# Second half of the w_out product by seven block products: a fused attention and gated-MLP layer on one core

## The chip, the cores and the metric

The kernel runs on one core of one Trainium2 chip. The metric is the device time of one execution in microseconds (us), from start to end on that core; a lower one is better. The time before is the median of four runs. A profile of one execution, taken by the hardware profiler, shows where that time goes: each instruction on each engine with its start and its length, and for an engine that sat idle, what it waited for.

The engines are named as in the profile: PE is TensorE (matmul), PEld its weight load, DVE is VectorE, ACT is ScalarE, POOL is GpSimd, SP is SyncE, which here only issues DMAs. A name with a q, such as ACTq, is the queue of that engine when it issues a DMA.

## The reference

One layer of a sequence model: a block A with linear-memory attention, then a block B with a spatially gated MLP. S is 2048 tokens, D is 1024 features, F is 3584, Fh is 1792. All inputs and the output are bf16. The change lies in the last line of block B alone.

```python
h  = x + A(layernorm(x), wq, wk, wv, wo, beta)
z  = gelu(layernorm(h) @ w_in)                  # [2048, 3584]
z1 = z[:, :1792]
z2 = layernorm(z[:, 1792:])
g  = w_sp @ z2 + b_sp[:, None]                  # w_sp: [2048, 2048], over tokens
h2 = h + (z1 * g) @ w_out                       # w_out: [1792, 1024]
```

## The kernel before

**How the order is made.** The kernel writes out its program by hand. Each call such as `pe.matmul(...)`, `dve.tensor_tensor(...)` or `sp.dma_start(...)` goes through a recorder. It appends the instruction to that engine's own queue, in the order of the calls, and works out from the memory that each instruction touches which semaphores it must wait for. So each engine runs its queue strictly in the order written, and an instruction that waits holds up what stands behind it on that engine. All instructions but the launch carry one source line, the recorder's L210; they are told apart by the names of their tiles.

**Seven products.** A product of two matrices that are each cut into 2 x 2 blocks needs eight block products. It can be done with seven, if sums and differences of blocks are multiplied and the seven results are combined (the scheme of Winograd). The kernel before does this for part of the z1 projection and for both halves of the gate product w_sp @ z2. It works with fp16 operands, scaled by powers of two so that sums of blocks stay within range.

**The stages at the end of the kernel**, which are what the change touches:

1. *Gate 0*, `gate(0)`: the gate for tokens 0 to 1023. It has 7 groups g; each is a block of 128 of the 896 features of one half of Fh. A group needs seven products of 8 matmuls with 512 columns: with `b11` (helper `p1`), `b21` (`p2`), `t2`, `t1`, `t3`, `t4` and `b22`. Four operand sums per group, `ss(1..4, g)`, 128x1024 in fp16 on DVE, fill the four parts of the tile `ss` through `s_sum`. They exist once, not twice.
2. *The 16 units*: 16 calls of `out_unit` for tokens 0 to 1023. Each multiplies 14 chunks of z1T with half of w_out's columns (14 matmuls of 512 columns), adds the residual, which was loaded into a `fin` tile from where h was stored, and stores the result. Loads and stores of `fin` are issued from ACT's queue. Meanwhile the transposed blocks of w_sp for gate 1 are loaded by SP and are scaled and summed on DVE (`sp_half`, `sp_sum`).
3. *Gate 1*, `gate(1)`: the same for tokens 1024 to 2047. At its beginning, the second half of w_out's columns is loaded into the part of z1T that the units have left, a DMA of 1.8 MB on SP.
4. *Last units*: 16 further units (the last one cut into 384 and 128 columns) for tokens 1024 to 2047, with `fin` loads and stores on SP's queue.

**Inside a group of the gate.** The banks of PSUM are used so that products are added onto one another: `t2` goes to bank `bb`, DVE reads it (`u2 = bank * scale + s1b2`), then `t3` is added onto it and DVE reads again (`u3`), then `t4` is added and DVE reads a third time (`s1b1`). So the `t3` product must wait until DVE has read u2, and `t4` until DVE has read u3. Bank `bc` takes `t1`, then `b22`. PE's order in a group is t2, t1, (p1 of group g+2 if 1 <= g <= 3), t3, then p2 of the next group (p1 of group 6 in group 5, p2 of group 6 in group 6), t4, b22. DVE's order is u2, ss(1, g+1), ss(2, g+1), u3 twice, `out`, ss(3, g+1), `c11`, s1b1, `out`, u2 again for `bc`, `out`, ss(4, g+1). Here `out` multiplies a finished gate block with its block of z1T and writes the result back into z1T as bf16. `copy1` on ACT takes the p1 product out of its bank, and POOL adds the bias rows `brow` to it, twice per group (tile `tmp_s1b`).

**Scales.** `scale_of` turns squares that ACT has summed (`SQ`, `accum_out`) into one factor: a cast to bf16 on POOL into the tile `SQB`, a small matmul with ones (`ONES`) that sums over the 128 partitions, then a few one-column steps on DVE and a power of -1/2 on POOL, cut to a power of two. The name `TOT` stands for the total and `INV[0]` for the inverse of the gate's scale.

Of the kernel before, what the change touches and what calls it, by code (L numbers as in the profile page):

```python
# [5 lines left out]
BF16 = mybir.dt.bfloat16  # L6
F16 = mybir.dt.float16
F32 = mybir.dt.float32
I32 = mybir.dt.int32
ACTF = mybir.ActivationFunctionType  # L10
ALU = mybir.AluOpType

T = 2048
# [5 lines left out]
FH = 1792  # L19
NTC = T // 128  # L20
# [238 lines left out]
def bass_sequential_preLN__memory_aug_infini_attn__mixer_gmlp__prompt_kernel(  # L259
# [15 lines left out]
    out2d = out[0]  # L275
    R = _Recorder(nc)
    pe, act, dve, pool, sp = R.pe, R.act, R.dve, R.pool, R.sp

    K = 1024
# [4 lines left out]
    def tens(name, shape, dt, off):  # L284
        sz = int(np.prod(shape[1:])) * mybir.dt.size(dt)
        assert off % 32 == 0 and off + sz <= ARENA, (name, off, sz)
        t = nc.alloc_sbuf_tensor_at(name, list(shape), dt, offset=abase + off)
        R.space[t[:].tensor.name] = ("sbuf", off)
        return t

    class Bump:
# [4 lines left out]
        def __call__(self, name, shape, dt):  # L296
# [68 lines left out]
    Z2H = tens("z2h", [128, NTC, FH], F16, 134 * K)  # L365
    Z1T = tens("z1T", [128, 14, T], BF16, 62 * K)
    ROLES = (("b11", 14), ("b12", 22), ("b22", 46), ("b21", 126))
    RAW = {k: tens(k + "r", [128, 8, L], BF16, o * K) for k, o in ROLES}
    BH = {k: tens(k + "h", [128, 8, L], F16, o * K)
          for k, o in ROLES + (("t1", 118), ("t2", 190), ("t3", 22), ("t4", 38))}  # L370
    SS = tens("ss", [128, 4, 8, 128], F16, 30 * K)
    Z1X = tens("z1x", [128, 14, T], F16, 62 * K)
# [6 lines left out]
    b3 = Bump(dead, 4 * K)  # L379
# [4 lines left out]
    ONES = b3("ones", [128, 128], BF16)  # L384
    MHZ = b3("mhz", [128, 1], F32)
    SQ = b3("sq", [128, 16], F32)
    SQZ = b3("sqz", [128, 14], F32)
    SQB = b3("sqb", [128, 16], BF16)
    TOT = b3("tot", [128, 1], F32)
    TOP = b3("top", [128, 1], F32)  # L390
    SC = [b3("sc%d" % i, [128, 1], F32) for i in range(2)]
    INV = [b3("inv%d" % i, [128, 1], F32) for i in range(2)]
    TMP = {k: tens("tmp_" + k, [128, L], F32, (4 + 2 * i) * K)
           for i, k in enumerate(("s1", "s1b1", "s1b2", "u2", "u3"))}
    SJ = [tens("sj%d" % i, [128, T], BF16, (4 + 4 * i) * K) for i in range(2)]
    BROW = [tens("brow%d" % i, [128, L], BF16, (205 + i) * K) for i in range(2)]
    WO0 = [tens("w_out0%d" % i, [128, 7, 512], BF16, o * K) for i, o in enumerate((54, 198))]
    WO1 = [tens("w_out1%d" % i, [128, 7, 512], BF16, o * K) for i, o in enumerate((30, 4))]
    FIN = [tens("fin%d" % i, [128, 512], BF16, o * K) for i, o in enumerate((37, 11, 12, 13))]

    PS = nc.alloc_psum_tensor("ps", [128, 8, 512], F32)
    R.space[PS[:, 0, :].tensor.name] = ("psum", 0)

    def bank(b):
        return PS[:, b, :]
# [7 lines left out]
    def next_bank():  # L413
        b = rot["banks"][rot["n"] % len(rot["banks"])]
        rot["n"] += 1
        return b
# [367 lines left out]
    for t in range(4):  # L784
        for h in range(2):
            pe.matmul(PS[:, br, t * 128:(t + 1) * 128], RSB[:, h, t:t + 1].to_broadcast([128, 128]), IDENT[:],
                      start=(h == 0), stop=(h == 1))
# [53 lines left out]
    for n in range(LAST + 1):  # L841
        s, c = divmod(n, NQ)
        f1, f2, f3, f4 = [], [], [], []
        if n < LAST:
            f1, f2 = [("qk", n + 1, 1)], [("qk", n + 1, 0)]
# [24 lines left out]
        if s < NSEG - 1 and 0 <= c - 2 * (s == 0) < 4:  # L870
            t = c - 2 * (s == 0)
# [112 lines left out]
    def at(q, f, *a):  # L984
        aux.setdefault(q, []).append((f, a))

    for r in range(16):
        q = (37 * r + 15) // 16
        at(q, sp_norm, r)
        if r < 14:  # L990
            at(q, sp_norm_load, r + 2)
    at(37, pool.tensor_copy, SQB[:], SQ[:])
    for k in range(12):
        at(k + 1, wz_norm, (1, 2, 0)[k // 4], k % 4)
    for k in range(8):
# [54 lines left out]
    def sp_sum(o, r=None, eng=dve):  # L1050
        a, b = SUMS[o]
        s = slice(0, 8) if r is None else slice(2 * r, 2 * r + 2)
        eng.tensor_tensor(BH[o][:, s, :], BH[a][:, s, :], BH[b][:, s, :], ALU.subtract)

    def a_blk(i, j, g):
        f = 896 * i + 128 * g
        return Z2H[:, 8 * j:8 * j + 8, f:f + 128]
# [11 lines left out]
    def prod(b, a, w, first):  # L1069
        for i in range(8):  # L1070
            pe.matmul(bank(b), a[:, i, :], BH[w][:, i, :], start=(first and i == 0), stop=(i == 7),
                      skip_group_check=True)

    def gate(pr, seam=lambda: None, mid=lambda: None):
        t1, t2 = slice(1024 * pr, 1024 * pr + 512), slice(1024 * pr + 512, 1024 * pr + 1024)
        s1, s1b1, s1b2, u2, u3 = (TMP[k][:] for k in ("s1", "s1b1", "s1b2", "u2", "u3"))

        def stt(o, b, add):
            dve.scalar_tensor_tensor(o, bank(b), INV[0][:], add, ALU.mult, ALU.add)

        def out(v, g, i, t):
            z = Z1T[:, g + 7 * i, t]
            dve.tensor_tensor(z, v, z, ALU.mult)

        def ss(k, g):
            if g < 7:
                s_sum(k, g)

        def p1(g):
            prod(g % 3, a_blk(0, 0, g), "b11", True)  # L1090

        def copy1(g):
            act.activation(s1, bank(g % 3), ACTF.Copy, scale=INV[0][:])

        def p2(g):
            prod(g % 3, a_blk(0, 1, g), "b21", False)

        def c11(g):
            stt(u3, g % 3, BROW[0][:])
            out(u3, g, 0, t1)  # L1100

        p1(0)
        copy1(0)
        pool.tensor_tensor(s1b2, s1, BROW[1][:], ALU.add)
        pool.tensor_tensor(s1b1, s1, BROW[0][:], ALU.add)
        p1(1)
        p1(2)
        seam()
        p2(0)
        c11(0)  # L1110
        for g in range(7):
            bb, bc = 3 + g % 2, 5 + g % 2
            prod(bb, SS[:, 1], "t2", True)
            prod(bc, SS[:, 0], "t1", True)
            stt(u2, bb, s1b2)
            if g == 0:
                mid()
            ss(1, g + 1)
            ss(2, g + 1)
            if 1 <= g <= 3:  # L1120
                p1(g + 2)
            prod(bb, SS[:, 2], "t3", False)
            if g < 5:
                copy1(g + 1)
                p2(g + 1)
            elif g == 5:
                p1(6)
                copy1(6)
            else:
                p2(6)  # L1130
            stt(u3, bb, s1b2)
            stt(u3, bc, u3)
            out(u3, g, 1, t2)
            if g < 6:
                pool.tensor_tensor(s1b2, s1, BROW[1][:], ALU.add)
            ss(3, g + 1)
            if g != 5:
                c11(min(g + 1, 6))
            prod(bb, a_blk(1, 1, g), "t4", False)
            stt(s1b1, bb, s1b1)  # L1140
            out(s1b1, g, 1, t1)
            if g < 6:
                pool.tensor_tensor(s1b1, s1, BROW[0][:], ALU.add)
            prod(bc, SS[:, 3], "b22", False)
            stt(u2, bc, u2)
            out(u2, g, 0, t2)
            ss(4, g + 1)

    fins = {}

    def fin_load(u, q=sp):
        tc, lo, w = u
        k = len(fins) % 4
        fins[u] = FIN[k]
        q.dma_start(FIN[k][:, 0:w], out2d[tc * 128:(tc + 1) * 128, lo:lo + w])

    def out_unit(u, wsl, q=sp):
        tc, lo, w = u
        b = next_bank()
        mm8(PS[:, b, 0:w], lambda i: Z1T[:, i, tc * 128:(tc + 1) * 128], wsl, n=14)  # L1160
        fin = fins[u]
        dve.tensor_tensor(fin[:, 0:w], fin[:, 0:w], PS[:, b, 0:w], ALU.add)
        q.dma_start(out2d[tc * 128:(tc + 1) * 128, lo:lo + w], fin[:, 0:w])
# [81 lines left out]
    units = [(tc, 0, 512) for tc in range(6)] + [(tc, 512, 512) for tc in range(8)] + [(tc, 0, 512) for tc in (6, 7)]  # L1245
    def seam():
        sp_half("b21")
        for k in range(1, 5):
            s_sum(k, 0)

    def mid():
        for r in range(4):
            sp_sum("t4", r)

    gate(0, seam, mid)
    fin_load(units[0], act)
    fin_load(units[1], act)
    for k in ("b11", "b12", "b22", "b21"):
# [2 lines left out]
    brow_load(1)  # L1261
    for i in range(2):
        act.dma_start(WO1[i][:], wout[:, 7 * i:7 * i + 7, 512:D])
    for n, u in enumerate(units):
        if n + 2 < 16:
            fin_load(units[n + 2], act)
        out_unit(u, (lambda i: WO0[i // 7][:, i % 7, :]) if u[1] == 0 else
                 (lambda i: WO1[i // 7][:, i % 7, :]), act)
        if n == 1:
            sp_half("b11")  # L1270
        if n == 4:
            sp_half("b12")
            sp_sum("t1")
        if n == 6:
            sp_half("b22")
            sp_sum("t3")
        if n == 8:
            sp_sum("t2")
        if n == 10:
            sp_half("b21")  # L1280
            sp_sum("t4")
        if n == 13:
            for k in range(1, 5):
                s_sum(k, 0)

    sp.dma_start(Z1T[:, :, 0:512], wout[:, :, 512:D])
    gate(1)
    units = [(tc, lo, 512) for tc in range(8, NTC) for lo in (0, 512)]
    units[-1:] = [(NTC - 1, 512, 384), (NTC - 1, 896, 128)]
    fin_load(units[0])  # L1290
    fin_load(units[1])
    for n, u in enumerate(units):
        if n + 2 < len(units):
            fin_load(units[n + 2])
        tc, lo, w = u
        out_unit(u, (lambda i: WO0[i // 7][:, i % 7, 0:w]) if lo == 0 else (lambda i: Z1T[:, i, lo - 512:lo - 512 + w]))

    R.emit()

# [27 lines left out]
```

## Time and profile before

| | |
|---|---|
| median of 4 runs | 766.82 us (766.7 to 767.25) |
| profiled execution: time, span | 766.91 us, 765.1 us |
| granted TensorE clock | 1.00 |
| gate 0 | 494.7 to 580.0 us of the span |
| 16 units | 580.0 to 628.3 us |
| gate 1 | 628.3 to 714.1 us |
| last units to the end | 714.1 to 765.1 us |

The span reaches from the first to the last instruction on the core; the execution's own time is 1.8 us longer than its span. The four stages together make 270.4 us, a third of the span. Each row of a timeline has its start in us from the span's beginning, its length in us, the engine, the operation, the tiles that it writes and reads, the shape (partitions x elements) and the number of instructions merged into the row. In brackets at the end stands how long the engine was idle before and what released it. Lengths of pipelined matmuls overlap; the distance between two starts is what a matmul costs.

### The profile page before, as it was taken

What the parts mean: (1) busy time and instruction counts of PE and PEld (TensorE: products, weight loads), DVE (VectorE), ACT (ScalarE), POOL (GpSimd) and SP (SyncE); (2) the same over time, 40 slices, a digit from 0 to 9 for tenths busy, and PEclk for the clock granted to TensorE, in tenths of its full rate; (3) what the DMA queues carried; (4) which work ended last, traced back from release to release, by engine and by line L of the source; (5) the groups of instructions that cost most, each with busy time, mean ns of one, the idle gap of its engine ahead of it and who ended that gap; (6) DMA issues with size and microseconds to landing.
All of it is one profiled execution on the core that took longest, in us unless ns stands there. A gap on an engine that the chain in (4) does not pass through costs nothing.

```text
span 765.1 us, 13399 instructions
## 1 busy us (share of the span) xinstructions
PE 754.7 (99%) x5496; PEld 360.6 (47%) x5496; DVE 542.8 (71%) x961; ACT 369.9 (48%) x429; POOL 274.6 (36%) x426
## 2 busy tenths in 40 slices
PE   8999999999999999999999999999999999999998
PEld 3445455555554445455554444444444444444444
DVE  5585589768974575759876986998884666788422
ACT  6777877787777668136984789600000000000000
POOL 2564456555654333000069987421120002112000
PEclk9999999999999999999999999999999999999999
DMA  9554546354425231877630045400039850000222
GB/s 302 166 161 90 94 70 143 83 88 95 97 57 132 76 71 43 209 203 234 193 111 1 0 80 100 119 33 1 0 56 162 235 195 1 1 0 1 63 82 76
DMA packets 138078, 75.08 MB, mean 98 GB/s; under 512 B 98336, under 2 KB 128800, under 8 KB 138016
## 3 DMA queue, kind: packets, MB, share of 16 engines
q1 hardware_dynamic: 130768, 67.40, 36.4%
q10 hardware_dynamic: 7248, 6.82, 3.2%
q8 instruction: 43, 0.70, 0.4%
q14 instruction: 19, 0.16, 0.1%
HBM read 42.74 MB, written 8.39 MB: 67 GB/s over the span
## 4 chain that ended last, share of the span: by engine, by line
PE 80%; DVE 7%; ACT 4%; DMA 3%; issue 3%; POOL 2%; POOLq 0%; DVEq 0%; ACTq 0%
PE ps L210 80%; ACT sj L210 3%; DVE tmp_u L210 2%; DMA sj<-in_B_w_sp_dram 2%; DVE ss L210 1%; ACT z L210 1%; DVE zt L210 1%; POOL sz L210 1%; POOL zrs L210 1%; DVE z1T L210 1%; DMA wv<-in_A_wv_dram 1%; DVE tmp_s1b L210 0%; DVE t4h L210 0%; DVE t2h L210 0%; DVE ht L210 0%
## 5 line engine op out<-in xcount | busy, mean ns | idle before, releaser
L210 ACT ACTIVATE e<-ps 128x2048 bf16<-128x2048 f32 (+1 forms) x96 | 152.7, 1590 | 41.7 <-PE ps L210 41.5
L210 POOL TENSOR_SCALAR_AFFINE_SELECT e<-e 128x512 bf16<-128x512 bf16 x128 | 90.6, 720 | 132.3 <-ACT e L210 132.2
L210 ACT ACTIVATE tmp_s<-ps,inv 128x512 f32<-128x512 f32 x14 | 9.6, 686 | 195.6 <-POOL tmp_s1b L210 100.8
L210 POOL TENSOR_TENSOR tmp_s1b<-tmp_s,brow 128x512 f32<-128x512 f32 x28 | 34.0, 1218 | 184.1 <-ACT tmp_s L210 82.7
L210 PE MATMUL ps<-win,hnT 128*128 128x448 bf16 x512 | 98.4, 352 | 0.0
L210 PE MATMUL ps<-w_out,z1T 128*128 128x512 bf16 x336 | 74.0, 379 | 0.0
L210 PEld LDWEIGHTS ps<-win,hnT 128*128 128x128 bf16 x512 | 49.6, 98 | 46.3 <-issue 0.2
L210 DVE TENSOR_TENSOR fin<-fin,ps 128x512 bf16<-128x512 bf16 (+2 forms) x33 | 21.8, 669 | 56.8 <-PE ps L210 39.5
L210 PE MATMUL ps<-wv,xnT 128*128 128x512 bf16 x256 | 59.5, 380 | 2.0 <-DMA wv<-in_A_wv_dram 2.0
L210 PE MATMUL ps<-xnT,wk 128*128 128x512 bf16 x256 | 60.8, 380 | 0.0
L210 PE MATMUL ps<-xnT,wq 128*128 128x512 bf16 x256 | 60.5, 379 | 0.0
L210 PE MATMUL ps<-wo,oT 128*128 128x512 bf16 x256 | 58.0, 379 | 0.0
L210 DVE TENSOR_TENSOR zt<-ps,zt 128x512 f32<-128x512 f32 x70 | 47.4, 686 | 14.8 <-PE ps L210 12.2
L210 PEld LDWEIGHTS ps<-w_out,z1T 128*128 128x128 bf16 x336 | 32.9, 98 | 39.6
L210 ACT ACTIVATE z<-ps 128x448 bf16<-128x448 f32 x60 | 30.5, 547 | 34.7 <-PE ps L210 34.7
L210 PEld LDWEIGHTS ps<-v,e 128*128 128x128 bf16 x1280 | 38.8, 96 | 14.0 <-issue 6.5
L210 DVE BATCH_NORM_STATS2 zst<-z 128x6 f32<-128x448 bf16 x64 | 37.8, 608 | 9.0 <-ACT z L210 9.0
L210 PE MATMUL ps<-v,e 128*128 128x33 bf16 x1280 | 42.2, 178 | 0.0
L210 DVE RECIPROCAL rd<-ps 128x16 f32<-128x16 f32 x32 | 8.0, 251 | 47.1 <-PE ps L210 46.9
L210 ACT ACTIVATE z1T<-zt,inv 128x512 bf16<-128x512 f32 x42 | 29.7, 718 | 16.2 <-DVE zt L210 16.1
L210 PEld LDWEIGHTS ps<-wo,oT 128*128 128x128 bf16 x256 | 24.1, 98 | 27.5
L210 DVE TENSOR_TENSOR z1T<-tmp_u,z1T 128x512 bf16<-128x512 f32 x42 | 35.8, 853 | 1.4
(163 smaller groups left out, 1336.8 us busy)
## 6 DMA issues: line engine op xcount, KB each, us to landing
sj<-in_B_w_sp_dram SPq DMA_DIRECT2D x16, 512.0 KB, 3.5
xch<-in_A_x_dram SPq DMA_DIRECT2D x16, 256.0 KB, 3.5
xr<-in_A_x_dram SPq DMA_DIRECT2D x16, 256.0 KB, 4.0
out_dram<-hch SPq DMA_DIRECT2D x16, 256.0 KB, 2.4
win<-in_B_w_in_dram SPq DMA_DIRECT2D x4, 896.0 KB, 5.2
wz<-in_B_w_in_dram SPq DMA_DIRECT2D x6, 512.0 KB, 7.7
wo<-in_A_wo_dram SPq DMA_DIRECT2D x1, 2048.0 KB, 8.4
fin<-out_dram ACTq DMA_DIRECT2D x16, 128.0 KB, 3.4
```

Source lines behind the costliest of these rows:

```text
L210: ins = getattr(e, op.name)(*op.args, **op.kw)
```

## The change

The second half of the w_out product (tokens 1024 to 2047) goes from 224 matmuls to 4 groups of seven products with 7 matmuls each, 196 in all. Each matrix is cut 2 x 2: tokens into 512 and 512, the 14 chunks of Fh into 7 and 7, the columns of w_out into 512 and 512. A group g is 128 tokens of each half. What belongs to it:

- The gate's result in `gate(1)` is written as fp16 into `Z1X` (same memory as z1T), multiplied by a power of two, `YS`, which is folded into `INVY` and into the bias rows. The blocks of w_out are copied to fp16 with a power of two `SCW` by ACT during gate 1 (`ob_scale`, 8 copies), and `INVO` undoes both scales.
- The scales come from norms. 28 Squares of z1's second half run on ACT during gate 0 (`z1_norm`, with PSUM bank 7 as a dump); 8 Squares of w_out (`wo_norm`) and 2 of the bias rows (`brow_sq`) run on ACT between the units. `scale_y` runs behind unit 9 and `scale_w` behind unit 11; each has a small matmul in PE's queue.
- The sums of w_out blocks, `t1`, `t2` and `t3` in 12 pieces, run on DVE during gate 1 (`ob_sum`, called through `each1`); `t4` in four pieces in the first group of the last stage. The sums of gate blocks, `y_sum`, are four per group, 128x896; those of group 0 are split so that only the last chunk remains for after the gate.
- The residual is loaded as eight tiles `FIN2` of 128x1024; two of the adds per group that were residual adds become POOL adds onto the copied first product (`o_adds`).
- In both gates, `ss(4, g)` for a group is made in the group itself, behind u2, and no longer at the end of the group before. In group 0, `ss(1, 1)` and `ss(2, 1)` go behind the first `out`. `each(g, k)` is a hook with four places in a group: 0 ahead of t3, 1 ahead of u3, 2 ahead of s1b1, 3 at the end.

```diff
     def gate(pr, seam=lambda: None, mid=lambda: None, each=lambda g, k: None):
+        inv, zo = (INV[0], Z1T) if pr == 0 else (INVY, Z1X)
...
         def out(v, g, i, t):
-            z = Z1T[:, g + 7 * i, t]
-            dve.tensor_tensor(z, v, z, ALU.mult)
+            dve.tensor_tensor(zo[:, g + 7 * i, t], v, Z1T[:, g + 7 * i, t], ALU.mult)
...
             stt(u2, bb, s1b2)
             if g == 0:
                 mid()
-            ss(1, g + 1)
-            ss(2, g + 1)
+            ss(4, g)
+            if g:
+                ss(1, g + 1)
+                ss(2, g + 1)
             if 1 <= g <= 3:
                 p1(g + 2)
+            each(g, 0)
             prod(bb, SS[:, 2], "t3", False)
...
             out(u3, g, 1, t2)
+            if not g:
+                ss(1, 1)
+                ss(2, 1)
...
             stt(u2, bc, u2)
             out(u2, g, 0, t2)
-            ss(4, g + 1)
+            each(g, 3)
...
+    def total(n):
+        b = next_bank()
+        pe.matmul(PS[:, b, 0:n], ONES[:], SQB[:, 0:n], start=True, stop=True)
+        dve.tensor_reduce(out=TOT[:], in_=PS[:, b, 0:n], axis=mybir.AxisListType.X, op=ALU.add)
+        dve.tensor_single_scalar(TOT[:], TOT[:], 1e-30, ALU.max)
+
+    def power(o):
+        pool.tensor_tensor(TOP[:], TOT[:], MHZ[:], ALU.pow)
+        dve.tensor_single_scalar(TOP[:].bitcast(I32), TOP[:].bitcast(I32), 0x7F800000, ALU.bitwise_and)
+        dve.tensor_single_scalar(o[:], TOP[:], 8192.0, ALU.mult)
+
+    def scale_y():
+        total(28)
+        pool.tensor_single_scalar(TW[:], TW[:], float(2 * T * FH), ALU.mult)
+        for k in range(2):
+            pool.tensor_tensor(TW[:], TW[:], BSQ[:, k:k + 1], ALU.add)
+        pool.tensor_tensor(TOT[:], TOT[:], TW[:], ALU.mult)
+        power(YS)
+        dve.tensor_tensor(INVY[:], INV[0][:], YS[:], ALU.mult)
+        for k in range(2):
+            act.activation(BROW[k][:], BROW[k][:], ACTF.Copy, scale=YS[:])
...
     for n, u in enumerate(units):
...
+        if 1 <= n <= 8:
+            wo_norm(n - 1)
...
+        if n == 9:
+            brow_sq()
+            scale_y()
+            pool.tensor_copy(SQB[:, 0:8], SQY[:, 0:8])
...
+        if n == 11:
+            scale_w()
...
+    fin_in(2)
+    fin_in(3)
+    o_p1(0)
+    o_adds(0)
+    for x in range(1, 4):
+        y_sum(x, 0, 6, 7)
+    o_prod(3, o_s(2, 0), "t2", True, cs=range(6))
+    o_p2(0)
+    o_c11(0)
+    for g in range(4):
...
+        if g == 0:
+            o_prod(bc, o_s(1, g), "t1", True, cs=range(6))
+        cs = range(6, 7) if g == 0 else range(7)
+        o_prod(bb, o_s(2, g), "t2", True, cs=cs)
+        for b, lo, hi in last:
+            o_prod(b, o_s(1, g), "t1", True, lo, hi, cs)
+        o_stt(f12[:], bb, f12[:])
+        if g == 0:
+            ob_sum("t4", 0)
...
+        y_sum(4, g)
+        o_prod(bb, o_s(3, g), "t3", False)
+        if g < 3:
+            o_p1(g + 1)
+        elif g == 3:
+            o_p2(3)
+        o_stt(f22[:], bb, f22[:])
...
+        o_prod(bb, o_y(1, 1, g), "t4", False)
+        if 0 < g < 3:
+            o_p2(g)
+            o_c11(g)
+        o_stt(FIN2[:, g, 1, 0, :], bb, f21[:])
+        fin_out(g, 1, 0)
+        for b, lo, hi in last:
+            o_prod(b, o_s(4, g), "b22", False, lo, hi)
+            o_stt(FIN2[:, g, 0, 1, lo:hi], b, f12[:, lo:hi], lo, hi)
+            fin_out(g, 0, 1, lo, hi)
```

In the last stage, f12, f22 and f21 are the names of the steps by which DVE reads a bank of the product (`o_stt`); `o_p1`, `o_p2` and `o_c11` play the roles of `p1`, `p2` and `c11`.

## The prediction

> **What bounds the kernel now.** I read the shares first, then the table by stage, the waits of TensorE (PE), and the order of time inside a group. The page's first part and its chain of waits:
>
> ```profile
> PE 754.7 (99%) x5496; PEld 360.6 (47%) x5496; DVE 542.8 (71%) x961; ACT 369.9 (48%) x429; POOL 274.6 (36%) x426
> PE 80%; DVE 7%; ACT 4%; DMA 3%; issue 3%; POOL 2%; POOLq 0%; DVEq 0%; ACTq 0%
> ```
>
> PE is the bound, and VectorE (DVE) the only other engine with a large share of the chain. The stages that the change touches, from the table by windows (gate 0; 16 units; gate 1; last units):
>
> ```profile
> 494.70:580.00 85.30, 83.61 (x386) 37.26 (x385) 74.57 (x104) 5.64 (x9) 17.66 (x14) 1.00 0.17 39
> 580.00:628.34 48.34, 48.34 (x225) 21.91 (x224) 27.59 (x30) 0.00 (x0) 0.00 (x0) 1.00 0.88 217
> 628.34:714.13 85.79, 84.95 (x393) 38.17 (x392) 66.45 (x93) 4.81 (x7) 16.36 (x14) 1.00 0.01 3
> 714.13:765.10 50.97, 48.55 (x239) 22.68 (x237) 12.79 (x20) 0.00 (x0) 0.00 (x0) 1.00 0.27 83
> ```
>
> The columns are length, then busy time and count of PE, PEld, DVE, ACT, POOL, then clock, DMA share, GB/s. The unit stage is pure PE: 48.34 us for 224 matmuls, 0.2158 us each, so a product of 8 costs 1.727 us and one of 7 costs 1.51. Both gates have DVE nearly as full as PE; in the last stage DVE is idle three quarters of the time. DMA is 0.88 busy in the unit stage.
>
> The timeline at gate 1's group 4 shows what the gates wait for:
>
> ```profile
> 682.72 0.74 DVE L210 SCALAR_TENSOR_TENSOR tmp_u<-ps,inv,tmp_u 128x512 f32<-128x512 f32 x1
> 683.50 1.09 DVE L210 TENSOR_TENSOR z1T<-tmp_u,z1T 128x512 bf16<-128x512 f32 x1
> 684.51 0.68 DVE L210 TENSOR_TENSOR ss<-z2h,ss 128x1024 f16<-128x1024 f16 x1
> 685.11 0.74 DVE L210 SCALAR_TENSOR_TENSOR tmp_u<-ps,inv,tmp_s1b 128x512 f32<-128x512 f32 x1
> 685.90 1.90 PE L210 MATMUL ps<-t3h,ss 128*128 128x512 f16 x8 [0.42 <-DVE tmp_u L210]
> ```
>
> The t3 product adds onto a bank that DVE must first have read as u2 (row 685.11). It could start at 683.60 + 1.727 = 685.33, so it loses 0.57. Directly ahead of u2 stands the fourth operand sum.
>
> **The skill.** (1) "TensorE: Matmul & The Clock Gate", Back-to-back issue gap: about 216 ns for 512 columns; the trace has 215.8, it agrees. (2) "VectorE: DVE Perf Modes", perf-mode tier table: a 16-bit tensor_tensor in SBUF goes at twice the fp32 rate. It agrees: 1024 fp16 elements take 0.68 us, 512 fp32 ones 0.69. (3) "SBUF — State Buffer": a DVE instruction with two SBUF inputs contends with a GpSimd one that reads SBUF. It agrees: the z1T row above lasts 1.09 beside POOL's tmp_s1b, 0.69 without. (4) "Perfetto Trace Analysis", DVE / Act Engine Instruction: the sequencer goes on once an instruction is in the wait queue; a DMA issue waits on the sequencer. The trace has ACT's second row below running beside the first:
>
> ```profile
> 0.80 1.28 ACT L210 ACT_TABLE_LOAD   x1 [0.80 <-PEq L1312]
> 1.26 0.97 ACTq L210 DMA_DIRECT2D wv<-in_A_wv_dram  x2
> ```
>
> **Part 1, gate 0: the fourth sum moved behind u2, two sums of group 0 moved behind `out`.** Groups 4 and 5 each lose 0.59 at t3 (551.76 against 549.44 + 1.727 = 551.17; 562.72 against 562.13). With the 0.6 of ss(4) behind u2, u2 ends at its due time: -1.2. In group 0, t3 comes 0.24 late and t4 0.93 late (507.99 against 503.60 + 3.45), 1.17 in all, since u3 stands behind four t4h sums and two ss. Now it stands behind four and one, and the seam has one sum less: u3 ends about 506.65, t4 is due at 506.81. Next late is u2 of group 1: 515.6 against 515.4, +0.2. The 28 new Squares on ACT (0.63 + 0.2 for the accumulator each, by the junk rows) have 3.3 us in a group of 12.1 where ACT uses 0.7; `copy1` behind them has 5 us to spare. Sum **-2.1** (-2.5 to -1.0).
>
> **Part 2, the unit stage.** Added: eight Squares of 1792 on ACT (1.7 + 0.2 by the 2048-wide sj row of 1.92), two scale chains, two tiny matmuls (under 0.1 together). The second matmul is the danger: it stands in PE's queue behind unit 11, due 580.0 + 168 x 0.2158 = 616.3, and needs POOL's second cast into sqb, which POOL does after the first scale's `pow`. That needs the Squares of `brow_sq`, which ACT's queue has behind the store of unit 9. Where that store is now:
>
> ```profile
> 610.41 0.38 SPq L210 DMA_DIRECT2D z1T<-in_B_w_out_dram  x1
> 610.79 0.35 ACTq L210 DMA_DIRECT2D out_dram<-fin  x1
> 613.48 0.68 DVE L210 TENSOR_TENSOR fin<-fin,ps 128x512 bf16<-128x512 bf16 x1
> 615.56 0.34 ACTq L210 DMA_DIRECT2D fin<-out_dram  x1
> 615.94 0.44 ACTq L210 DMA_DIRECT2D out_dram<-fin  x1
> ```
>
> Row 610.79 stores unit 7 and takes 4.7 us to land beside the 1.8 MB load of 610.41; only then is its buffer free for unit 11's load (615.56), and only behind that goes unit 9's store (615.94). Then: two brow Squares, 616.4 + 2 x 0.85 = 618.1; POOL add and multiply about 0.3 each (tensor_scalar on one column takes 0.26), pow 0.58 and cast 0.2 by their rows, with gaps: 619.6; PE at 619.7. PE loses **3.4**, and everything behind it in PE's queue moves. Not below 0; the upper end, if ACT's Squares hold up its DMA issues, is in rival B. Behind it nothing more is late: DVE waits for the pow up to 619.4, so unit 10's add moves from 617.9 to 619.9 and unit 15's to 632, while gate 1's first product needs only banks freed by 625. With the matmuls: **+3.5** (+0.5 to +6).
>
> **Part 3, gate 1.** The fourth sum leaves the path to u2, but 12 sums of w_out blocks enter, one behind the second operand sum and one at the group's end, in groups 1 to 6: pitch 0.61 at 1024 wide, 0.4 at 512. From u3 to the next u2 the trace has 676.89 to 685.11, 8.22 us without a gap; minus 0.6 plus 0.6 that stays. From u2 to u3 DVE now needs 0.66 + 0.61 + 0.71 + 0.61 + 0.61 = 3.2, against 2.73 until PE delivers. In groups 1 to 3 (seven products, 12.09 us) DVE's 11.5 fits. Group 4's t3 stays 0.57 late, group 5's, from u2 to u2, comes after 3.2 + 8.04 (its closing sum is a narrow one) and u2's own 0.8, PE after 0.8 + 6 x 1.727 = 11.16: 0.88 late (was 0.58), group 6 catches up without `c11`. Sum **+0.3** (-0.6 to +1.5). `ob_scale` puts 8 copies (about 2 us) on ACT, which used 4.8 of 85.8 us.
>
> **Part 4, last stage.** 7 x 4 x 7 = 196 matmuls instead of 224: -28 x 0.2158 = -6.04. New waits: the first t3 needs f12 read after t2's seventh chunk; only one short matmul lies between, so 0.75 + 0.05 are open: +0.8. The first t4 needs f22, and DVE has the four t4 sums (2.3) and a y sum (0.6) ahead of it: f22 ends at 3.65 after f12 where PE comes at 3.0: +0.65. Later groups: six stt of 0.77 and four sums of 0.6 to 0.9 make 8 us of DVE in 10.6 of PE; +0.3 for POOL's adds beside them. The y sums of group 0's last chunk have 5.6 us of PE work as cover (p1, t2, p2, t1). On SP 8 loads and 17 stores replace 17 and 17; the loads start in group 6, over 10 us ahead of use. Sum **-4.3** (-5.2 to -2.5). The end: the store of 128 columns comes behind two more DVE steps: **+0.2**.
>
> **Sum.** -2.1 + 3.5 + 0.3 - 4.3 + 0.2 = -2.4. The profiled execution took 766.91 (span 765.1, 1.8 around it), 0.09 above the median of 766.82; so 764.5, on the median **764.4**.
>
> **Rivals.** B, ACT works strictly in turn: from unit 2's store at 598.05, seven Squares of 1.9 and seven pairs of issues of 0.8 put unit 9's store at 617.5; if its load falls beside the 1.8 MB one (6.7 us for the load at 611.18) at 618.7. PE then waits 4.4 to 6.1: 765.4 to 767.1, middle 766.3. For it: ACT's issue row at 585.59 lasted 5.06. Against it: the rows at 0.80 and 1.26. C, no wait at the second scale: brow's Squares would have to run by 614.6, so the stores of units 7 to 9 must land in the 1.7 to 2.1 us seen at 606 and 607. Then -2.1 + 0.1 + 0.3 - 4.3 + 0.2 = -5.8: 761.0. D, slower: the new 16-bit sums fall to the fp32 rate (1.2 for 1024) through their wide rows in z1x. A DVE group of gate 1 then has 10.3 + 2.4 = 12.7 us and decides from 12.09 on: about 1.2 in groups 1 to 3, 2.3 in 4 to 6; in the last stage the t4 and y sums add 2.5: 764.4 + 6 = 770.4. Against it: ss sums read 128-element pieces from eight rows and keep 0.68. That the 28 matmuls do not go can't be: the program has 196.
>
> **Numbers.** A measurement here tells about 0.2%, 1.5 us, from no change: faster means under 765.3, slower over 768.4. My case 0.62 (762.6 to 765.9, of it 0.53 faster), B 0.15 (same), C 0.13 (faster), D 0.10 (slower). Faster 0.66, same 0.24, slower 0.10. The range 761.0 to 767.2 takes in A, B and most of C.
>
> **What would show it.** Stage lengths: gate 0 83.2, units 51.9 with one PE gap of 3 to 4 us ahead of a 128x8 matmul on sqb, released by POOL; gate 1 86.1, PE waits at t3 of groups 4 and 5; last 46.9, two gaps in its first group. Wrong if that gap is missing or over 5, if the sums into z1x take over 0.8, or if gate 1 exceeds 88.

## The result, and the profile after

The changed kernel takes **764.36 us** (median of 43 runs, 761.62 to 771.71) against 766.81 for the kernel before, measured beside it (63 runs, 765.18 to 768.91). The ratio is 0.9979, 95% interval 0.997 to 0.9989. The prediction said 764.4, in 761.0 to 767.2.

The two sets of times differ in more than their middle. The kernel before stays within 3.7 us; the changed one spreads over 10. The experiments below show where much of that spread comes from.

The profiled execution of the changed kernel took 762.86 us, span 761.1. First the busy times and the chain of waits of its page:

```profile
PE 750.7 (99%) x5470; PEld 357.8 (47%) x5470; DVE 576.3 (76%) x1016; ACT 422.7 (56%) x519; POOL 294.4 (39%) x447
PE 76%; DVE 11%; ACT 4%; issue 3%; POOL 3%; DMA 3%; ACTq 0%; DVEq 0%; POOLq 0%
```

PE is busy for 4.0 us less, and DVE's share of the chain has gone from 7% to 11%: PE waits for DVE in more places. The same stages by windows (gate 0; units; gate 1; last units; columns as before):

```profile
492.98:578.11 85.13, 85.02 (x393) 38.06 (x392) 76.80 (x106) 26.42 (x66) 18.71 (x17) 1.00 0.18 42
578.11:626.79 48.68, 48.57 (x228) 21.89 (x226) 28.40 (x40) 17.10 (x22) 1.83 (x6) 1.00 0.84 217
626.79:713.09 86.30, 85.12 (x393) 38.13 (x392) 73.97 (x106) 18.23 (x15) 16.20 (x14) 1.00 0.08 27
713.09:761.10 48.01, 43.20 (x211) 19.60 (x209) 37.33 (x52) 2.75 (x4) 16.84 (x12) 1.00 0.14 44
```

From first matmul to first matmul, gate 0 went from 87.00 us (493.00 to 580.00) to 85.13. The table:

| stage | before | after | measured | predicted |
|---|---|---|---|---|
| gate 0 | 87.00 | 85.13 | -1.87 | -2.1 |
| units | 48.34 | 48.68 | +0.34 | +3.5 |
| gate 1 | 85.79 | 86.30 | +0.51 | +0.3 |
| last units with the end | 50.97 | 48.01 | -2.96 | -4.1 |
| sum | | | -3.98 | -2.4 |

So the execution that was profiled is not the one that the prediction described: the large wait of the unit stage is missing in it, and the last stage gains less. The timeline at the second scale, rows of the cast and of the small matmul:

```profile
614.42 0.19 POOL L210 CAST sqb<-sqy 128x8 bf16<-128x8 f32 x1
614.67 0.18 PE L210 MATMUL ps<-sqb,ones 128*128 128x8 bf16 x1
```

The cast ended 36.5 us after the units' start (578.11), where 39.6 were predicted. PE came to the small matmul at about 614.4 and lost some 0.2 us.

What PE waits for from gate 0 to the end (columns: us in total, times, longest):

```profile
PE ps L210 <- DVE tmp_u L210: 1.2, 3, 0.6
PE ps L210 <- DVE sy L210: 1.0, 1, 1.0
PE ps L210 <- DVE ot L210: 0.9, 1, 0.9
```

The first row is the t3 product of groups 4, 5 and 6 in gate 1. The other two lie in the first group of the last stage, whose timeline is the most telling part of the profile after:

```profile
715.57 4.10 POOL L210 TENSOR_TENSOR ot<-ot,fin 128x512 f32<-128x512 f32 x3 [11.26 <-ACT ot L210]
716.12 1.38 DVE L210 TENSOR_TENSOR z1x<-z1x 128x512 f16<-128x512 f16 x1
717.42 1.24 DVE L210 SCALAR_TENSOR_TENSOR sy<-z1x 128x128 f16<-128x128 f16 x1
718.69 1.12 DVE L210 SCALAR_TENSOR_TENSOR sy<-sy,z1x 128x128 f16<-128x128 f16 x1
719.74 0.28 DVE L210 SCALAR_TENSOR_TENSOR sy<-z1x 128x128 f16<-128x128 f16 x1
719.87 0.60 PE L210 MATMUL ps<-z1x,sy 128*128 128x512 f16 x2 [1.00 <-DVE sy L210]
721.39 1.68 PE L210 MATMUL ps<-z1x,sy 128*128 128x512 f16 x7 [0.92 <-DVE ot L210]
```

POOL's row holds the three adds of `o_adds` (three per group, not two as the description of the change has it). DVE's first row is the last sum of w_out blocks, and the three 128x128 sums behind it are the y sums of group 0's last chunk. The third of these, which runs after POOL's adds (715.57 + 4.10 = 719.67), takes 0.28 us; the first two, beside them, take 1.24 and 1.12. PE stands still for 1.00 until the second of them is done, then for 0.92 until DVE has read f12.

### The profile page after: what moved, and what is told of

Its sections match the earlier page's. It is cut to its first block, busy times and chain, and to the rows that moved or that the text cites. A ratio compares the mean times of both kernels' runs of the same rounds, so it can differ in the third digit from the quotient of the medians.

```text
span 761.1 us, 13511 instructions
## 1 busy us (share of the span) xinstructions
PE 750.7 (99%) x5470; PEld 357.8 (47%) x5470; DVE 576.3 (76%) x1016; ACT 422.7 (56%) x519; POOL 294.4 (39%) x447
## 3 DMA queue, kind: packets, MB, share of 16 engines
q1 hardware_dynamic: 129472, 67.40, 36.5%
## 4 chain that ended last, share of the span: by engine, by line
PE 76%; DVE 11%; ACT 4%; issue 3%; POOL 3%; DMA 3%; ACTq 0%; DVEq 0%; POOLq 0%
PE ps L210 76%; ACT sj L210 2%; DVE tmp_u L210 2%; DMA sj<-in_B_w_sp_dram 2%; DVE z1x L210 2%; DVE ss L210 2%; POOL zrs L210 1%; DVE zt L210 1%; POOL sz L210 1%; ACT z L210 1%; DMA wv<-in_A_wv_dram 1%; DVE fin L210 1%; DVE sy L210 1%; DVE t2h L210 0%; DVE z1T L210 0%
## 5 line engine op out<-in xcount | busy, mean ns | idle before, releaser
L210 ACT ACTIVATE z<-ps 128x448 bf16<-128x448 f32 x60 | 30.4, 544 | 34.4 <-PE ps L210 34.4
L210 PE MATMUL ps<-w_out,z1T 128*128 128x512 bf16 x224 | 48.7, 379 | 0.0
L210 ACT ACTIVATE tmp_s<-ps,invy 128x512 f32<-128x512 f32 x7 | 4.8, 687 | 65.4 <-POOL tmp_s1b L210 36.9
L210 PEld LDWEIGHTS ps<-xnT,wk 128*128 128x128 bf16 x256 | 22.6, 98 | 29.9 <-issue 5.0
L210 PEld LDWEIGHTS ps<-wv,xnT 128*128 128x128 bf16 x256 | 23.2, 98 | 27.7 <-DMA wv<-in_A_wv_dram 1.2
L210 POOL TENSOR_TENSOR sz<-wzh 128x512 f16<-128x512 f16 x28 | 33.0, 1178 | 8.2 <-PE ps L210 8.2
```

What stands on the lines that cost most here:

```text
L210: ins = getattr(e, op.name)(*op.args, **op.kw)
```

## The experiments

The first four kernels ran on one chip beside the kernel before (median 766.57, 30 runs), the other four on another one (766.86, 27 runs). Rows and windows come from one profiled execution each.

### e1: the changed kernel again

The edit: none. Is the 3.4 us wait of the prediction there in other executions?

> The changed kernel itself, to see its spread on the same chip as the others. Theory W (PE's wait for the second scale behind unit 11 differs from execution to execution with the landing of DMAs): a median near 764.4 us, single times spread over some 8 us. Rival K (the granted clock drops in some executions whatever the wait): the same spread, but also in every other kernel of this batch that has the new last stage.

Measured: 766.13 us (22 runs, 761.59 to 771.24), ratio 0.9998 (0.998 to 1.0016). The execution that was profiled took 768.09, and it has the wait. Its timeline, ACT's queue and what follows from it:

```profile
609.68 0.35 ACTq L210 DMA_DIRECT2D out_dram<-fin  x1
...
614.71 0.33 ACTq L210 DMA_DIRECT2D fin<-out_dram  x1
615.08 0.44 ACTq L210 DMA_DIRECT2D out_dram<-fin  x1
615.63 0.63 ACT L210 ACTIVATE t4h<-brow 128x512 f16<-128x512 bf16 x1 [1.68 <-DMA out_dram<-fin]
...
618.51 0.19 POOL L210 CAST sqb<-sqy 128x8 bf16<-128x8 f32 x1
618.75 0.18 PE L210 MATMUL ps<-sqb,ones 128*128 128x8 bf16 x1 [3.23 <-POOL sqb L210]
```

This is the chain of the prediction: the store of 609.68 (unit 7) frees its buffer late, so unit 11's load is issued at 614.71, only then unit 9's store (615.08), then the Squares of `brow`, the cast that ends at 618.70, which is 39.4 us after the units' start at 579.29, and PE waits 3.23. The unit stage took 51.59 (predicted 51.9), while gate 0 (85.35) and gate 1 (86.31) are close to those of the other execution. Of the 5.2 us between the two executions the unit stage makes 2.9, the last stage 1.1 (see e3), gate 0 0.2; 1.0 lies before gate 0.

What follows: the same program can have the wait or be almost free of it. Of these 22 runs 11 lie between 761.5 and 765.1 and 11 between 767.1 and 771.3, with nothing in between. But the 43 runs of the result fill that gap (nine of them lie between 765.3 and 767.1), so it is not shown that there are just two kinds of execution. The medians 764.36 and 766.13 are one program with different shares of shorter and longer executions. One thing that differs is when the loads of units 2 and 3 arrive; why is not known. In the profile of the result their residual add starts 15.1 us after the units' start (593.19), here 17.0 (596.25), in the kernel before 17.3 (597.33), and in the other seven profiles between 15.0 and 17.5.

### e2 and e3: the second scale two units later, one unit earlier

```diff
-        if n == 11:
+        if n == 13:        # e2;  e3: n == 10
             scale_w()
```

> scale_w behind unit 13 and no longer behind unit 11. PE reaches its small matmul 6 us later. W: the wait is gone in nearly all executions, the median falls by 2 us to about 762.3 and the long times (over 766) go. K: median 764.4 and the same long times.

> scale_w behind unit 10. PE reaches its small matmul 3 us earlier, at about 611.5, while the cast that it needs came at 614.6 in the profile of the changed kernel. W: a PE gap of 3 us or more ahead of the 128x8 matmul in every execution, median 766.5 to 768. K: no change against the changed kernel.

Measured: **e2 764.13** (7 runs, 761.97 to 765.1), ratio 0.9963 (0.995 to 0.9977), units 48.18 in a span of 760.2, no wait on `sqb`, and no run above 765.1; the median is 2.0 below that of e1, as expected, but not at the expected 762.3. **e3 771.4** (6 runs, 769.38 to 774.42), ratio 1.0055 (1.0041 to 1.0069), slower than the 766.5 to 768 that were expected. The profiled execution of e3 is the slowest of its six; its small matmul:

```profile
620.76 0.19 PE L210 MATMUL ps<-sqb,ones 128*128 128x8 bf16 x1 [7.90 <-POOL sqb L210]
```

The wait is the scale's and moves with its place in PE's queue: moved up by one unit, 3.0 us of PE's work, it goes from 3.23 to 7.90 (in this execution the cast also ended 1.6 us later, 41.0 after the units' start at 579.65), and moved back by two units it is gone. The windows of e3 at the gap and just behind it show something more in the clock column:

```profile
612.80:620.70 7.90, 0.07 (x1) 0.00 (x0) 1.53 (x5) 3.23 (x6) 1.27 (x5) 0.74 0.76 262
620.70:625.00 4.30, 4.24 (x15) 1.74 (x16) 4.20 (x6) 1.33 (x2) 0.01 (x1) 0.68 0.30 97
```

The clock granted to PE is 0.74 in the gap and 0.68 after it; the next 70 matmuls took 16.41 us instead of 70 x 0.2158 = 15.11. In e1's gap of 3.2 us it stayed at 1.00:

```profile
615.40:618.70 3.30, 0.12 (x1) 0.00 (x0) 0.11 (x1) 1.44 (x4) 1.28 (x5) 1.00 0.85 296
```

But e1 has a fall of the clock elsewhere, in the first group of its last stage, behind PE's stops of 1.00 and 0.92 us. Three rows of PE and the window of the fall:

```profile
725.49 2.49 PE L210 MATMUL ps<-z1x,sy 128*128 128x512 f16 x7 [0.92 <-DVE ot L210]
727.77 2.60 PE L210 MATMUL ps<-w_out0h,z1x 128*128 128x512 f16 x7
730.21 1.67 PE L210 MATMUL ps<-z2h,z1x 128*128 128x512 f16 x7
...
726.22:729.63 3.41, 3.41 (x10) 1.23 (x9) 3.38 (x7) 0.00 (x0) 0.00 (x0) 0.50 0.00 0
```

From start to start the first two products took 2.28 and 2.44 us instead of 1.51, and the last stage 49.1 us instead of 48.0. In e3 the same happened there (49.2). In the profile after, in e2, e5 and e7 the same two stops cost no clock.

The Trainium skill, "TensorE: Matmul & The Clock Gate", Part 1: The HAM clock gate, says that the clock is halved after an idle window of some 3.4 us and comes back after a busy one, and that the windows run freely. The traces agree in part: every stretch at 0.50 inside e1, e3 and e7 lasts 3.41 us or twice that, and e3's gap of 7.90 us brought one. They differ in that PE need not be idle for a whole window. Counted in steps of 3.41 us from these stretches, PE was busy for at most 1.53 us in the step ahead of each of the four (e3 0.00 and 1.49, e1 1.49, e7 1.53 near its beginning). In every other step at full clock of these three executions, between PE's first and last matmul, it was busy for 1.60 us or more (1.60 in e7's last stage, 1.94 and 1.66 in e1's gap of 3.23, which lies across two steps). So where a stop falls among the steps matters, and not its length alone; that the steps run on unbroken between the stretches is assumed, and fits e3, whose two falls are 116.05 us apart, 34 steps.

One such stretch makes a run's mean clock 0.998 (half of 3.41 us in 766), wherever it lies. In e1 10 of the 11 runs above 767 us have 0.995 to 0.998, of those below 3 have 0.998, and all 30 runs of the kernel before beside them have 1.00. What each of the long runs has of the wait and of the low clock was not seen, since only one execution is profiled.

### e4: the new order of operand sums alone

The kernel before, with only the last point of the change, in both gates:

```diff
-            ss(1, g + 1)
-            ss(2, g + 1)
+            ss(4, g)
+            if g:
+                ss(1, g + 1)
+                ss(2, g + 1)
...
             out(u3, g, 1, t2)
+            if not g:
+                ss(1, 1)
+                ss(2, 1)
...
             out(u2, g, 0, t2)
-            ss(4, g + 1)
...
-            for k in range(1, 5):      # in seam and behind unit 13
+            for k in range(1, 4):
                 s_sum(k, 0)
```

> The kernel before with the new order of the operand sums in both gates and nothing else. Theory of part 1: gate 0 is 1.9 us shorter as in the changed kernel, and gate 1, which has no block sums here, loses both waits at t3 (1.15 us): 3.0 us in all, 763.8 us. Rival: the sums only move the wait to u3, which then comes late: under 1 us.

Measured: **763.83** (7 runs, 763.21 to 765.87), ratio 0.9964 (0.9952 to 0.9977). Its windows (gate 0; units; gate 1):

```profile
494.81:580.15 85.34, 85.18 (x393) 38.18 (x393) 76.99 (x107) 6.86 (x10) 17.66 (x14) 1.00 0.18 42
580.15:628.28 48.13, 47.92 (x219) 21.84 (x223) 26.98 (x28) 0.00 (x0) 0.00 (x0) 1.00 0.84 218
628.28:713.10 84.82, 84.82 (x393) 38.21 (x392) 67.46 (x94) 4.81 (x7) 16.36 (x14) 1.00 0.01 2
```

No wait of PE is left inside either gate. Gate 0 is as long as with the whole change, and gate 1 is 84.8, 1.0 less than before and 1.5 less than in the changed kernel.

What follows: this small edit alone, with no new product, is worth 2.7 us, as much as the whole change on its median (-2.45), and more than the whole change on this chip (e1, ratio 0.9998). Gate 0's gain comes from the order of the sums.

### e5: the second scale behind the last unit

```diff
-        if n == 11:
-            scale_w()
...
+        if n == 15:
+            scale_w()
```

> scale_w behind the last unit, 12 us later in PE's queue than in the changed kernel. Theory W: no execution waits for the second cast any more; what is left is gate 0 -1.7, gate 1 +0.5, last stage -3.0, so 4.2 us under the kernel before, about 762.4 us, with single times no wider apart than those of the kernel before (3 us). Rival: the median stays at the 764 of the version with the scale behind unit 13, since something else in the units varies.

Measured: **763.15** (6 runs, 762.16 to 763.54), ratio 0.9942 (0.992 to 0.9963). Units 48.19, gate 1 86.30, last 48.03. The wait is gone, the spread is 1.4 us, and nothing takes the wait's place: PE's waits are those of the profile after (tmp_u 1.2, sy 1.0, ot 0.9). The loads came late here too: unit 2's add starts 17.2 us after the units' start and the first Square of `brow` 36.7 (e1: 17.0 and 36.3), and nothing was lost by it. Against e4, the products with all that belongs to them then bring 1.0 us by the two ratios (-3.7 against -2.7), whose intervals overlap; by the stages it is 48.03 against 50.97 in the last one, less 86.30 against 84.82 in gate 1, about 1.5.

### e6: e5, with POOL's first adds held back behind the short sums

A one-column copy on POOL, which reads the last column of the third y sum, stands ahead of `o_adds(0)`:

```diff
-    o_adds(0)
     for x in range(1, 4):
         y_sum(x, 0, 6, 7)
+    pool.tensor_copy(TW[:], SY[0][:, 2, 6, 0:1])
+    o_adds(0)
```

> As the version with the scale behind the last unit, and POOL's three residual adds of the last stage's first group are held, by a copy of one column, until DVE has made the three short sums of the last chunk. Theory C (contention: the short sums took 1.24 and 1.12 us for 128 elements because POOL's adds ran beside them, 0.28 without): PE's wait of 1.0 us for sy goes, the last stage becomes 1.0 us shorter, median 761.4. Rival: the short sums are slow by themselves (their form), no change; or the adds now come late and PE waits as long for f12.

Measured: **762.35** (6 runs, 760.77 to 763.77), ratio 0.9931 (0.9909 to 0.9954); last stage 47.72 instead of 48.03, 0.3 us where 1.0 had been expected. The timeline of the same place:

```profile
717.24 0.28 DVE L210 SCALAR_TENSOR_TENSOR sy<-z1x 128x128 f16<-128x128 f16 x1
717.56 0.29 DVE L210 SCALAR_TENSOR_TENSOR sy<-sy,z1x 128x128 f16<-128x128 f16 x1
...
718.26 3.38 POOL L210 TENSOR_TENSOR ot<-ot,fin 128x512 f32<-128x512 f32 x3
...
720.66 3.06 DVE L210 TENSOR_TENSOR z2h<-w_out0h,z1x 128x1024 f16<-128x1024 f16 x4
720.80 1.69 PE L210 MATMUL ps<-z1x,sy 128*128 128x512 f16 x7 [0.71 <-DVE ot L210]
...
724.97 1.69 PE L210 MATMUL ps<-z2h,z1x 128*128 128x512 f16 x7 [0.98 <-DVE ot L210]
```

With POOL out of the way the short sums take 0.28 and 0.29, and PE's wait for `sy` is gone. That POOL's adds stretched them is shown. The gain is small because the adds now lie beside the four t4 sums, which take 3.06 instead of 2.21: t4 waits 0.98, where it had been some 0.3 late. The contention moved; it did not go.

### e7: the 1.8 MB load later

The second scale at unit 11 as in the change, but the load of w_out's second half behind unit 12 on ACT's queue instead of ahead of gate 1 on SP's, so its queue changes with its place:

```diff
+        if n == 12:
+            act.dma_start(Z1T[:, :, 0:512], wout[:, :, 512:D])
...
-    sp.dma_start(Z1T[:, :, 0:512], wout[:, :, 512:D])
     gate(1, each=each1)
```

> The changed kernel, scale_w behind unit 11 as there, but the 1.8 MB load into z1T is issued on ACT's queue behind unit 12 and not beside the stores of units 7 to 9. If that load is what holds these stores: unit 9's store leaves 1.5 to 2 us earlier, PE's wait for the second cast falls to at most 1.5, median 763. Rival: the delay comes from the transposed loads at the beginning of the units; then the wait and its spread stay, median 764.4 to 766.

Measured: 765.34 (22 runs, 762.16 to 768.73), ratio 0.9976 (0.9963 to 0.9988). In its profiled execution (766.40) unit 9's store is issued 34.1 us after the units' start and the wait is 1.68:

```profile
617.34 0.18 PE L210 MATMUL ps<-sqb,ones 128*128 128x8 bf16 x1 [1.68 <-POOL sqb L210]
```

In e1 it was 35.8 and 3.23. But the median is that of the rival (764.4 to 766) and not the expected 763, the spread is still 6.6 us, and these are two single executions whose loads also arrived at different times (unit 2's add at 16.4 here, 17.0 in e1). So the load's share of the delay is not shown.

All the profiles together say more. In the others the 1.8 MB load is issued 30.2 to 30.4 us after the units' start. Where unit 7's store goes out ahead of it, the store lands in 1.7 (the profile after, e6), 1.8 (e2, e4) or 3.3 us (e8); where it goes out behind it, in 4.7 (before), 5.0 (e1), 5.2 (e5) and 6.1 (e3). The late stores are thus those behind the load. But in e7, with no such load near, the store took 3.9 us, so the load is not the only thing that holds it.

### e8: e5 without the sums of w_out blocks in gate 1

```diff
-        for n, (o, h) in enumerate([(o, h) for o in ("t1", "t2", "t3") for h in (0, 2, 4, 6)]):
+        for n, (o, h) in enumerate([(o, h) for o in () for h in (0, 2, 4, 6)]):
```

> As the version with the scale behind the last unit, but the 12 sums of w_out blocks in gate 1 are left out (the last stage multiplies with b22 and b12 in their place), to price them. Theory: they are what leaves PE's three waits at t3 in groups 4 to 6; gate 1 goes from 86.3 to 84.7, median 760.8. Rival: the waits come from fp16 writes of the gate or from ACT's copies; then gate 1 stays at 86.3.

Here t1, t2 and t3 of the w_out blocks are not made, and their products read existing tiles. Measured: 760.29 (6 runs, 759.97 to 762.95), ratio 0.9913 (0.9892 to 0.9934). Gate 1 took 84.84, with no wait inside it, as in e4. The twelve sums cost 86.30 - 84.84 = 1.5 us there, though DVE has 12 us of free time in that stage. The medians of e5 and e8 differ by more, 2.9; by the profiles 0.4 lies in the last stage, and the rest is not located. In the last stage the wait for `sy` is gone as well: the short sums still take 1.13, 1.13 and 1.24 us beside POOL's adds, but no sum of blocks stands ahead of them. PE then waits 1.75 for f12.

## Why the prediction was right, and where not

The number was right, 764.4 against 764.36. That they agree so closely is partly luck: the wait was 3.2 us in one execution and 0.2 in another, the median depends on how many have it, and on the chip of e1 it was 766.13. In the profiled execution two terms are off in opposite directions, the units (+0.34 for +3.5) and the last stage (-2.96 for -4.1).

**Part 1, gate 0: right.** -1.87 in the profiled execution and 85.3 in e1, e2, e4 and e5 (-1.7), predicted -2.1. No wait remains inside gate 0. e4 shows that the two moves in the order do this.

**Part 2, unit stage: the mechanism was right, the size is not one value.** In e1 each step of the chain is there, with the cast done 39.4 us after the units' start against 39.6 and the wait 3.23 against 3.4. In the profiled execution after, the same chain ended 2.9 us earlier and cost 0.2. The prediction gave "no wait" a chance of its own (rival C, 0.13); if the runs below 766 us are those without it, which was not seen, it is half or more (28 of 43, 11 of 22). The step that failed is the reading of landing times from one execution as the kernel's own: unit 7's store took 4.7 us to land in the kernel before, and 1.7 in the profile after. A second cost was missed: stops of PE can also lower its clock behind them (e3: 1.3 us more behind the gap; e1: 1.1 in the last stage).

**Part 3, gate 1: right in place, a little low.** +0.51 against +0.3; by e4 and e8 this is -1.0 from the order of the sums and +1.5 from the sums of w_out blocks. Groups 4 and 5 wait at t3 as foreseen, 0.58 and 0.75 late (predicted 0.57 and 0.88). "Group 6 catches up" was wrong; the profile after has the three rows:

```profile
684.35 1.90 PE L210 MATMUL ps<-t3h,ss 128*128 128x512 f16 x8 [0.42 <-DVE tmp_u L210]
...
695.48 1.90 PE L210 MATMUL ps<-t3h,ss 128*128 128x512 f16 x8 [0.60 <-DVE tmp_u L210]
...
706.18 1.90 PE L210 MATMUL ps<-t3h,ss 128*128 128x512 f16 x8 [0.16 <-DVE tmp_u L210]
```

**Part 4, last stage: the matmuls went, one term was mis-sized.** From the first matmul to the last product, 189 matmuls took 43.64 us (713.09 to 756.73) where 189 x 0.2158 = 40.8 are due, so 2.8 of waits stand against 1.75 predicted:

| wait | predicted | measured |
|---|---|---|
| t1's last chunk, for the y sums | 0 | 1.2 |
| first t3, for f12 | 0.8 | 1.1 |
| first t4, for f22 | 0.65 | 0.3 |
| later groups | 0.3 | 0.25 |

The failed step is the sentence that these y sums "have 5.6 us of PE work as cover". The cover was there, but the sums stand on DVE behind the gate's last `out` and the last sum of w_out blocks. From the start of that sum to the end of the second y sum it took 3.7 us (716.12 to 719.81), with POOL's adds beside them, and 1.0 in e6 without (716.90 to 717.85). Either alone was covered: e6, with the adds held back, and e8, without the block sum, have no wait for `sy`. The contention rule was quoted in the prediction and used for wide rows; it was not applied to the shortest instructions in the program, where it costs most in proportion. The end cost about +0.25, as predicted (+0.2).

**The rivals.** B, ACT strictly in turn, is refuted by the profile after, in which ACT's queue issues a load 0.05 us after a Square of 1.70 us began:

```profile
594.45 1.70 ACT L210 ACTIVATE t4h<-w_out 128x1792 f16<-128x1792 bf16 x1 [5.69 <-DVE fin L210]
594.50 0.39 ACTq L210 DMA_DIRECT2D fin<-out_dram  x1
```

C is what that execution shows. D, the slower end, is refuted: a sum of 1024 into `z1x` takes 0.68 (such as the row at 686.14), not 1.2.

**Where the expected gain went.** 28 matmuls less are 6.04 us. Of these, 2.8 are lost again in the last stage, 0.2 at the end, 1.5 in gate 1 for the sums (e8), and 0.3 to 3.2 in the unit stage of the two executions profiled. What remains of the products is about 1.2 in the profiled execution and 1.5 in e5; the order of the operand sums brings more, 1.7 in gate 0 and 1.0 in gate 1. The best measured version with the whole computation is e6, 762.35, whose interval overlaps that of e5 (763.15).

## What to carry to other kernels

An early consumer in an in-order queue turns a late DMA into idle time of the main engine: put a small matmul on a value that hangs on DMA landings as late as its own consumers allow (e2: the same scale two units later, ratio 0.9963 against e1's 0.9998 on the same chip; e5: four units later, 0.9942 on another, with six runs within 1.4 us where e1's 22 spread over 10). Measure each part of a combined change alone, since here a small change of order was worth as much as the whole. When a sum of instructions is said to be covered, look at what POOL runs beside it at that moment, for the short instructions above all. A stop of PE can cost more than its length, so two short stops close together are worth removing too (e1's last stage: 1.1 us of clock behind stops of 1.00 and 0.92).

## What was not expected of the hardware

A DVE instruction of 0.28 us (128x128 in fp16) took 1.12 to 1.24 beside POOL adds of 1.2 to 1.6 each, four times as long, while one of 1024 elements went from 0.68 to 1.64 at the worst. The single records show when it ends: in e8 POOL's adds end at 717.66, 718.82 and 719.98, and the three short sums at 717.81, 718.97 and 720.13; in the profile after, 718.51 and 719.67, and 718.66 and 719.81. Each of the five ends 0.15 us after an add. That fits waiting for the end of the running add, whatever the instruction's own length, and not a slower pace beside it.

A PE gap of 7.90 us lowered the granted clock to 0.74 and 0.68 in the windows at and behind it and cost 1.3 us beyond the gap. A gap of 3.23 us did not, but two stops of 1.00 and 0.92 us within 2.6 us did in e1 and e3, for 3.41 us at 0.50, and did not in four other executions.
